# Attention and an MLP on one core: two tiles of batch 0 as block products, values in 64 rows, and another hand-written order

## The chip, the cores and the metric

One core of a Trainium2 chip runs the kernel. The metric is the device time of one launch in microseconds (us); 406.1 us is the median of three runs of the kernel before (405.66 to 406.52).

## The reference

Cosine attention over 8 batches of 12 heads, 448 tokens of 64 features each, and then a two-layer MLP over the 3584 tokens. The MLP's weights are 768 x 2048 and 2048 x 768.

```python
q_n = q / (np.linalg.norm(q, axis=-1, keepdims=True) + 1e-06)
k_n = k / (np.linalg.norm(k, axis=-1, keepdims=True) + 1e-06)
scores = np.matmul(q_n, k_n.transpose(0, 1, 3, 2)) / tau
attn = softmax(scores)
x = np.matmul(attn, v)            # heads side by side: 3584 x 768
h = x @ w_in
g = h * np.clip(h + 3.0, 0.0, 6.0) / 6.0
out = g @ w_out
```

Inputs and output are float32; the matrix products run in bfloat16.

## The kernel before

**Pairs and tiles.** Two heads make a pair, 48 pairs in all, six to a batch. A raw tile j (0 to 47) holds the queries or the keys of two pairs: `load_qk` (line 187) fetches it through SP's DMA queue into a ring of seven buffers, and `raw_before` and `raw_buffer` (135 to 140) turn the ring into one of five from tile 26 on; the two buffers left over then hold intermediate results of the block products (`wide`). `square` (209) squares a tile on ScalarE, POOL or VectorE, `reduce` (226) sums the squares on VectorE, `norms` (244) makes 1/(|x| + 1e-6) of two tiles with four small ScalarE activations, and `normalise` (259) multiplies on POOL or VectorE. `vcast` (278) turns values into bfloat16. Tiles go through TensorE transposes (`transposes`, then copies of queries and keys, `copy_q`, `copy_k`, `copy_k3`) or, from tile 14 on, through the DMA crossbar (`crossbar`).

**Attention.** For a pair, `scores` (388) has four groups: three of two 64-row matmuls each (128 keys of either head), and a fourth for the last 64 keys of both heads. `exps` (421) runs the exponentials on ScalarE: up to pair 5 one instruction for both heads of a group (128 x 896), later one per bank (128 x 448). `values` (446) multiplies the exponentials with the values and a column of ones, eight matmuls of 65 columns a group. For the fourth group they read 64 rows from pair `FIRST` = 18 on, and 128 rows, half of which multiply zeros, before. `finish_values` (466) divides by the sum of the ones column, and `back`, `back_crossbar`, `back_two` bring the result into `xT`, the MLP's input.

**MLP.** `mm1_unit` (560) makes 128 of the 2048 hidden columns for a batch, with six matmuls of 448 columns; ScalarE then makes the gate and VectorE the product (line 581). 16 such units make g of one batch. `mm2_unit` (606) makes half of the output columns for 128 tokens with 16 matmuls of 384 columns. For most of the output a scheme of seven block products (Strassen's, in Winograd's form) takes the place of eight blocks: a pair of 128-token tiles is an entry of `PAIRS` (647), and `product_unit` (720) is one of its seven products, eight matmuls each. The scheme needs sums of blocks of g (`g_sum`, 699, VectorE), sums of blocks of `w_out` (`weight_sums`, 673: "1", "6" and "7" in buffers of their own; "y3" and "y4" written over `w_out` itself, so that ordinary units have to be through with it), and adds of the results on VectorE and POOL. Before, `second` (636) gives batch 0 six ordinary units, and `PAIRS` leaves out its first two tiles (`[1:]`).

**Order.** Each engine works its instructions in program order. Up to pair 17 that order is written out by hand in `PLAN` (line 21): a word is an operation, its number, and the engine (a, v, p for ScalarE, VectorE, POOL). "LQ" and "LV" load, "SQ", "RE", "NO", "NM" make the normalised tiles, "TR" transposes, "SC", "EX", "VA", "FI" are a pair's attention, "U" issues the next unit of a stream whose kinds `ORDER` (19) lists, "UA" and "UV" do the work of ScalarE and VectorE behind a unit, "W" issues one of eight weight DMAs on POOL's queue (the four parts of `w_in`, then the four of `w_out`), and "WS" makes weight sums. "D" and "DP" are fillers: matmuls on zeros into banks that nobody needs (`busy`, `busy_pv`, 913 and 918). From pair 18 on a loop issues the operations, with sums listed per pair in `side` (861). PSUM results from pair 6 on go round a ring of six banks (`next_bank`): a unit or score can start when the bank six places earlier has been read.

```python
for h in (range(2) if name == "M" else ["AB".index(name[0])]):
    rows = slice(64 * h, 64 * h + 64) if name == "M" and i >= FIRST else slice(0, 128)
```

Of the kernel before, what the change touches and what calls it, by code (L numbers as in the profile page):

```python
# [18 lines left out]
ORDER = "111111111111111111111111111111222222"  # L19

PLAN = [
# [40 lines left out]
def kernel(  # L62
# [72 lines left out]
    def raw_before(j):  # L135

        return j - NR if j < 26 else j - NR + 2

    def raw_buffer(j):
        return raws[j % NR if j < 26 else (j - 26) % (NR - 2)]  # L140
# [103 lines left out]
    def norms(d, *items):  # L244
# [11 lines left out]
        for x in items:  # L256
            issued.add(("NO", d, x))
# [185 lines left out]
    def q_cols(b, j):  # L443
        return slice(128 * j, 128 * j + 128)

    def values(i, g):
        needs(("VC", i), ("FI", i - 1), *values_after(i, g))
        at = at_of.pop((i, g))
        vt = vx[i % NVX]
# [643 lines left out]
```

## Time and profile before

| what | us |
|---|---|
| median of three runs | 406.1 |
| the profiled execution | 405.02 |
| its span, first to last instruction | 403.2 |
| first exponential starts | 12.11 |
| first unit of the hidden layer (line 566) starts | 42.09 |
| pair 18's first scores, where the loop starts | 114.64 |
| TensorE's busy share of the span | 98% |

A line of a group or of the timeline gives start and duration in us, the engine, the line of the kernel, the operation, output and inputs by name, shapes and how often; in square brackets stands how long the engine had been idle before, and whom it waited for. Matmuls are pipelined: the duration of one overlaps the next, so the cost of a group is read from its start to the next group's start. The clock column is the share of full speed that TensorE was granted, 1.00 throughout.

### The profile page before, as it was taken

The page shows a single profiled execution, that of the slowest core. Times are in us where ns is not written, and L with a number is a line of the kernel's source. Part 1 is how long each engine was busy: PE and PEld are TensorE (multiplying, and loading weights), DVE is VectorE, ACT ScalarE, POOL GpSimd, SP SyncE. Part 2 cuts the span into 40 slices and gives each one's busy share as a digit, 9 for nine tenths or more (in the row PEclk, how much of TensorE's full clock was granted, in tenths as well). Part 3 has the DMA queues.
Part 4 walks back from the last instruction along what each step waited for, and adds up shares of the span by engine and source line. Part 5 has one row for each costly group of instructions (what it writes and reads, how often), then busy time and mean ns, then how long its engine had stood idle before and what let it go on. Part 6 is the DMA issues. An engine that isn't in the chain of part 4 may idle for free.

```text
span 403.2 us, 9617 instructions
## 1 busy us (share of the span) xinstructions
PE 394.5 (98%) x3696; PEld 233.7 (58%) x3696; DVE 286.4 (71%) x501; ACT 266.2 (66%) x609; POOL 233.2 (58%) x228
## 2 busy tenths in 40 slices
PE   7999999999989999999999999999999999999996
PEld 5666556555655556555555556555565556555564
DVE  6898768766998676776857878687656666644663
ACT  6899998787557686776758768668648755224230
POOL 7899664562294996489386875776665500510070
PEclk9999999999999999999999999999999999999999
DMA  8999989989989559885989659986864523130133
GB/s 290 308 241 276 200 249 239 144 126 221 193 204 231 120 119 228 176 224 130 181 214 210 134 143 171 183 193 145 191 150 82 112 46 67 40 79 20 27 73 99
DMA packets 91566, 65.32 MB, mean 162 GB/s; under 512 B 56064, under 2 KB 89984, under 8 KB 91520
## 3 DMA queue, kind: packets, MB, share of 16 engines
q1 hardware_dynamic: 87408, 58.02, 62.8%
q0 software_dynamic: 3712, 6.29, 9.1%
q8 instruction: 29, 0.48, 0.5%
q10 hardware_dynamic: 400, 0.39, 0.3%
q14 instruction: 17, 0.14, 0.1%
HBM read 47.19 MB, written 11.01 MB: 144 GB/s over the span
## 4 chain that ended last, share of the span: by engine, by line
PE 94%; DVE 3%; DMA 1%; POOL 1%; ACT 0%; issue 0%; SPq 0%; DVEq 0%
PE M L566 24%; PE M L739 17%; PE PV L455 13%; PE Y L566 6%; PE M L415 6%; PE Z L566 5%; PE Y L739 4%; PE Z L739 4%; PE M L613 3%; PE M L819 2%; PE Z L415 2%; PE PV L921 2%; PE Z L819 1%; PE Y L415 1%; PE SC L415 1%; DMA big<-in_q_dram 1%
## 5 line engine op out<-in xcount | busy, mean ns | idle before, releaser
L433 ACT ACTIVATE at<-M 128x448 bf16<-128x448 f32 x200 | 99.6, 565 | 17.7 <-PE M L415 15.5
L566 PE MATMUL M<-xT,w_in_sb 128*128 128x448 bf16 x522 | 110.7, 353 | 0.0
L566 PEld LDWEIGHTS <-w_in_sb 128*128 128x128 bf16 x768 | 71.9, 98 | 62.5 <-issue 2.6
L267 POOL TENSOR_TENSOR nrm<-big,r 128x896 bf16<-128x896 f32 (+1 forms) x48 | 79.4, 1658 | 26.7 <-ACT r L255 18.5
L581 DVE SCALAR_TENSOR_TENSOR gT<-u,M 128x448 bf16<-128x448 bf16 x76 | 46.8, 618 | 35.6 <-ACT u L575 35.3
L455 PEld LDWEIGHTS <-at 128*128 128x128 bf16 (+1 forms) x1536 | 54.8, 97 | 24.1 <-issue 14.8
L224 POOL TENSOR_TENSOR big<-big 128x896 f32<-128x896 f32 (+3 forms) x39 | 63.8, 1639 | 8.0 <-DMA big<-in_k_dram 4.1
L575 ACT ACTIVATE u<-M 128x448 bf16<-128x448 f32 x87 | 48.8, 561 | 29.5 <-PE M L566 29.1
L455 PE MATMUL PV<-vx,at 128*128 128x65 bf16 (+1 forms) x1536 | 64.3, 194 | 0.2 <-DVE on L476 0.2
L236 DVE TENSOR_REDUCE n<-big 128x14 f32<-128x896 f32 (+1 forms) x50 | 51.8, 1040 | 3.9 <-ACT big L222 3.4
L372 POOL COPY km<-tT 64x128 bf16<-64x128 bf16 x34 | 12.4, 364 | 59.3 <-DMA tT<-nrm 43.4
L768 POOL TENSOR_TENSOR big<-big 128x384 f32<-128x384 f32 x11 | 12.0, 1088 | 55.1 <-ACT big L787 55.0
L739 PEld LDWEIGHTS <-gT 128*128 128x128 bf16 x288 | 27.8, 98 | 20.2 <-DVE gT L717 0.6
L739 PE MATMUL M<-w_out_sb,gT 128*128 128x384 bf16 x208 | 37.9, 326 | 0.1
L433 ACT ACTIVATE at<-Z 128x448 bf16<-128x448 f32 x49 | 27.6, 564 | 10.4 <-PE M L415 8.8
L286 POOL CAST vx<-big 128x512 bf16<-128x512 f32 x44 | 33.0, 754 | 2.4 <-DMA big<-in_v_dram 2.4
L476 DVE TENSOR_TENSOR on<-PV,rc 128x512 bf16<-128x512 f32 x48 | 33.2, 691 | 1.7
L415 PE MATMUL M<-tT,kz 64*128 64x448 bf16 (+1 forms) x175 | 31.9, 351 | 1.0 <-DVE o L626 1.0
L739 PEld LDWEIGHTS <-gs 128*128 128x128 bf16 x224 | 21.6, 98 | 14.5
L566 PE MATMUL Y<-xT,w_in_sb 128*128 128x448 bf16 x132 | 28.6, 353 | 0.0
L433 ACT ACTIVATE at<-Y 128x448 bf16<-128x448 f32 x45 | 25.6, 568 | 3.3 <-PE Z L415 3.1
L739 PE MATMUL M<-w_sum,gs 128*128 128x384 bf16 x144 | 26.3, 326 | 0.0
(131 smaller groups left out, 553.9 us busy)
## 6 DMA issues: line engine op xcount, KB each, us to landing
big<-in_v_dram SPq DMA_DIRECT2D x96, 128.0 KB, 4.7
big<-in_k_dram SPq DMA_DIRECT2D x24, 448.0 KB, 4.9
big<-in_q_dram SPq DMA_DIRECT2D x24, 448.0 KB, 4.3
out_dram<-o SPq DMA_DIRECT2D x107, 96.0 KB, 2.2
w_in_sb<-in_moe_w_in_dram POOLq DMA_DIRECT2D x4, 768.0 KB, 9.1
w_out_sb<-in_moe_w_out_dram POOLq DMA_DIRECT2D x4, 768.0 KB, 9.7
tT<-nrm SPq DMA_TRANSPOSE x34, 3.4
xT<-on SPq DMA_TRANSPOSE x25, 3.8
```

What stands on the lines that cost most here:

```text
L224: engines[e].tensor_tensor(out=o, in0=i, in1=i, op=ALU.mult)
L236: nc.vector.tensor_reduce(out=n2s[d % 2][:, j % 2, c], in_=sq[:, :, :, :].rearrange("p g c d -> p (g c) d")[:, c, :], axis=AX.X, op=ALU.add,)
L267: engines[e].tensor_tensor(out=nrm[:, :, g, :].rearrange("p c g d -> p g c d"), in0=raw_of[j][:, g, :, :], in1=rs[d % 2][3][:, j % 2, :] . ...
L286: (engines[e].copy if e == "a" else engines[e].tensor_copy)(out=o, in_=f)
L415: nc.tensor.matmul(o, ks, qt[rows], start=True, stop=True)
L433: nc.scalar.activation(out=o, in_=x, func=AF.Exp, scale=inv_tau)
L455: nc.tensor.matmul(pv_out(j, h), at[rows, n, q_cols(i // HP, j)], vt[rows, 3 + h if name == "M" else 5 * h + int(name[1]), :], start=(name ...
L476: nc.vector.tensor_tensor(out=on[:, :, :, :].rearrange("p j h d -> p h j d"), in0=pv4[:, :, :, 0:D], in1=rc[:, :, :].to_broadcast([128, 2, ...
L566: nc.tensor.matmul(ps[:, 0:S], w_in_sb[:, cc, fc * 128 : (fc + 1) * 128], x[:, cc, 0:S], start=(cc == 0), stop=(cc == CC - 1),)
L575: nc.scalar.activation(out=u[:, :], in_=ps[:, 0:S], func=AF.Relu, bias=0.5, scale=1.0 / 6.0)
L581: nc.vector.scalar_tensor_tensor(out=g[:, fc, c0 : c0 + S], in0=u[:, :], scalar=1.0, in1=ps[:, 0:S], op0=ALU.min, op1=ALU.mult,)
L739: nc.tensor.matmul(m, lhs[:, c, :], rhs[:, c, c0 : c0 + width], start=(base is None and c == 0), stop=(c == KC - 1), skip_group_check=True,)
```

## The change

**Products.** `PAIRS` gains the entry (batch 0, tiles 0 and 1), with the number -1 (`FOREMOST`). `second` now gives batch 0 two ordinary units (tile 2) and seven products of that pair. The sums of g for it are written in the plan ("GS"), the adds on POOL too ("UP").

**Values.** "VA" can carry "h": then the fourth group reads 64 rows. Eleven pairs have it: 1, 6 to 15.

**Norms.** "NA" and "ND" split `norms`: two activations on ScalarE, then an add and a reciprocal on VectorE. Five of the eleven norms of the plan are made so.

**Ring.** The raw ring shrinks to five buffers at tile 19 instead of 26, so that the space for the products' results is free earlier.

**Weight sums.** `weight_sums` can run on POOL; one half of "6" does. All are made in the plan; one half of "y4" was made in the loop (`side`, 18).

**Order.** `PLAN` is written anew. Before it has 10 D and 86 DP fillers, after 10 and 74; tiles 0 and 1 are squared by ScalarE alone; of the normalises of the plan VectorE does 2 before and 8 after, with one of the halves of tiles 0 and 1 each; copies and casts move between VectorE, POOL and ScalarE.

```diff
-ORDER = "111111111111111111111111111111222222"
+ORDER = "111111111111111111111111111111222222222"
...
-    "LQ.1 DP.5 SQ.1.a.11.3 SQ.1.p.4.3 DP.1 SQ.1.a.0.4 LQ.0 SQ.0.p.8.6 DP.2 DP.4 LQ.3 LQ.2 SQ.1.v.7.4 RE.1.1",
-    "SQ.0.a.0.6 RE.1.0 NO.0.1 LQ.5 LQ.4 SQ.0.v.6.2 DP.6 SQ.3.a.0.7 NM.1.p.0 D.10 RE.0.1 DP.3 NM.1.p.1 RE.0.0 DP.8",
-    "NO.0.0 LV.0 DP.2 SQ.2.a.0.7 NM.0.p.0 RE.3 RE.2 NM.0.p.1 TR.1.Y DP.2 TR.0.Z CK.0.v DP.4 SQ.4.p.0.7 CQ.0.v",
-    "SQ.5.a.0.7 LQ.6 NO.1 LV.1 LQ.7 SC.0.0.0 SC.0.1.1 DP.5 DP.3 CQ.1.v EX.0.0 RE.5 RE.4 NM.3.p SC.0.2.0 CK.1.v",
...
+    "D.10 LQ.1 LQ.0 DP.9 DP.2 SQ.1.a.0.2 DP.5 SQ.1.a.2.12 SQ.0.a.0.14 LQ.2 RE.1.0 RE.1.1 NO.0.1 LQ.3 DP.4 RE.0.1",
+    "RE.0.0 LQ.5 NM.1.v.0 NO.0.0 NM.0.v.1 SQ.3.a.0.7 NM.1.p.1 SQ.2.a.0.7 TR.1.Y DP.10 RE.3 LQ.4 CK.0.a NM.0.p.0",
+    "RE.2 SQ.5.a.0.7 TR.0.Z CQ.0.v LQ.6 SQ.4.p.0.7 DP.10 CK.1.v SC.0.0.0 NO.1 SC.0.1.1 EX.0.0 EX.0.1 DP.10 LV.0",
...
-    "CK.17.v XD.18 U EX.16.1 SQ.20.a.0.7 NM.19.p FI.15 WS.6 U UV XD.19 SC.16.3 RE.20 GL.0 WS.1 WS.7.0 EX.16.2 U VA.16.0 UA VA.16.1 LV.11",
-    "EX.16.3 SC.17.0 UV VC.19.p SC.17.1 SC.17.2 SQ.22.v.0.7 VA.16.2 LQ.23 EX.17.0 VA.16.3 EX.17.1 LV.10 U SC.17.3",
-    "XP.14 NO.10 FI.16 NM.20.p CK.18.v U CK.19.v WS.7.1 WS.y3 WS.y4.0 XB.16 EX.17.2 UV UA VA.17.0 VC.18.p EX.17.3 RE.22 CS.18.v",
...
+    "EX.13.1 UA UV NA.8 WS.6.p.0 SC.13.2 UV U UA SC.13.3 EX.13.2 FI.12 VC.14.a CK.14.v U ND.8 VA.13.0 UA U",
+    "NM.17.v UV VA.13.1 EX.13.3 UV W UA NM.16.p VA.13.2 CS.14.v UV SC.14.0 VA.13.3.h LQ.21 SC.14.1 EX.14.0 RE.18",
+    "U U EX.14.1 UA SC.14.2 CK.15.v NO.9 UA EX.14.2 SC.14.3 FI.13 U WS.7.v.0 EX.14.3 UV UV WS.7.v.1 UA VA.14.0",
+    "VC.15.a UV XD.16 VA.14.1 WS.1.v.0 LV.9 SC.15.0 SC.15.1 EX.15.0 U EX.15.1 CK.16.v WS.1.v.1 VA.14.2 XD.17 UA U",
+    "LV.8 GS.-1.6 UA U NM.18.p SC.15.2 EX.15.2 VA.14.3.h SC.15.3 UV SQ.21.a.0.7 WS.6.v.1 LQ.20 WS.y3.v.1 FI.14 UV",
+    "XP.12 CK.17.v U LV.10 UA SC.16.0 SC.16.1 WS.y3.v.0 EX.15.3 WS.y4.v.0 VA.15.0 VA.15.1 EX.16.0 U CS.16.v UA",
+    "VA.15.2 WS.y4.v.1 XD.18 UV VA.15.3.h SC.16.2 U GS.-1.5 EX.16.1 GS.-1.1 VC.17.a VC.16.v UA U GS.-1.2 NM.19.v",
...
-        return j - NR if j < 26 else j - NR + 2
+        return j - NR if j < 19 else j - NR + 2
...
-        return raws[j % NR if j < 26 else (j - 26) % (NR - 2)]
+        return raws[j % NR if j < 19 else (j - 19) % (NR - 2)]
...
+    def powers(d, *items):
+
+        needs(("NM", 2 * d - 4), ("NM", 2 * d - 3))
+        items = items or (0, 1)
+        for x in items:
+            needs(("RE", 2 * d + x))
+        it = slice(items[0], items[-1] + 1)
+        ln, nr = (t[:, it, :] for t in rs[d % 2][:2])
+        nc.scalar.activation(out=ln, in_=n2s[d % 2][:, it, :], func=AF.Ln)
+        nc.scalar.activation(out=nr, in_=ln, func=AF.Exp, scale=0.5)
+        for x in items:
+            issued.add(("NA", d, x))
+
+    def reciprocals(d, *items):
+
+        items = items or (0, 1)
+        for x in items:
+            needs(("NA", d, x))
+        it = slice(items[0], items[-1] + 1)
+        nr, le, r = (t[:, it, :] for t in rs[d % 2][1:])
+        nc.vector.tensor_scalar_add(out=le, in0=nr, scalar1=EPS)
+        nc.vector.reciprocal(out=r, in_=le)
...
-    def values(i, g):
+    def values(i, g, halves=""):
...
-                    rows = slice(64 * h, 64 * h + 64) if name == "M" and i >= FIRST else slice(0, 128)
+                    apart = name == "M" and (i >= FIRST or halves)
+                    rows = slice(64 * h, 64 * h + 64) if apart else slice(0, 128)
...
-        return [(mm2_unit, b, t, m) for m in (1, 0) for t in range(3)]
+        return [(mm2_unit, b, 2, m) for m in (1, 0)] + products(f"3.{FOREMOST} 4.{FOREMOST} 5a.{FOREMOST} 2a.{FOREMOST} 1.{FOREMOST} 6.{FOREMOST} 7.{FOREMOST}")
...
-    def weight_sums(what, c0, n):
+    def weight_sums(what, c0, n, e="v"):
...
-        nc.vector.tensor_tensor(out=o, in0=x, in1=y, op=op)
+        engines[e].tensor_tensor(out=o, in0=x, in1=y, op=op)
...
-        18: [(weight_sums, "y4", KC // 2, KC // 2)], 19: sums(0, "62"), 20: sums(0, "1"),
+        19: sums(0, "62"), 20: sums(0, "1"),
```

More of the change, by code (lines that the diff above doesn't have):

```diff
@@ L255, in norms @@
         nc.scalar.activation(out=r, in_=le, func=AF.Exp, scale=-1.0)
+        for x in items:
+            issued.add(("NO", d, x))
+    def powers(d, *items):
[11 more added lines that the diff above has]
+        items = items or (0, 1)
+        for x in items:
+            needs(("NA", d, x))
[3 more added lines that the diff above has]
+        nc.vector.reciprocal(out=r, in_=le)
         for x in items:
@@ L638, in second @@
         assert b % 2 == 0
-        return [(mm2_unit, b, t, m) for m in (1, 0) for t in range(3)]
+        return [(mm2_unit, b, 2, m) for m in (1, 0)] + products(f"3.{FOREMOST} 4.{FOREMOST} 5a.{FOREMOST} 2a.{FOREMOST} 1.{FOREMOST} 6.{FOREMOST} 7.{FOREMOST}")
     LEFT, RIGHT = slice(0, MH), slice(MH, 2 * MH)
-    PAIRS = [p for b in range(0, B, 2) for p in (((b, 0), (b, 1)), ((b + 1, 3), (b + 1, 0)), ((b + 1, 1), (b + 1, 2)))][1:]
-    LOOP = 8
+    PAIRS = [p for b in range(0, B, 2) for p in (((b, 0), (b, 1)), ((b + 1, 3), (b + 1, 0)), ((b + 1, 1), (b + 1, 2)))]
+    FOREMOST, LAST, LOOP = -1, len(PAIRS) - 2, 8
+    PAIRS = dict(enumerate(PAIRS, FOREMOST))
     summed, g_summed, issued_products = set(), set(), set()
@@ L657 @@
     wide = [big[:, c : c + MH] for c in range(0, 3 * MH, MH)]
-    wide_late = [tail(c, MH) for c in range(TAIL, TAIL + 2 * (len(PAIRS) - LOOP) * MH, MH)]
+    wide_late = [tail(c, MH) for c in range(TAIL, TAIL + 2 * (LAST + 1 - LOOP) * MH, MH)]
     def sum_of(n, what):
@@ L859 @@
     }
-    APART = {(n, y) for n in range(len(PAIRS)) for x, y in (("5a", "3"), ("2a", "4")) if f"{x}.{n}" in " ".join(TURNS.values()).split()}
+    APART = {(n, y) for n in PAIRS for x, y in (("5a", "3"), ("2a", "4")) if n == FOREMOST or f"{x}.{n}" in " ".join(TURNS.values()).split()}
     side = {
-        18: [(weight_sums, "y4", KC // 2, KC // 2)], 19: sums(0, "62"), 20: sums(0, "1"),
+        19: sums(0, "62"), 20: sums(0, "1"),
         21: sums(1, "75"), 22: sums(1, "621"),
@@ L946 @@
     OPS = {
-        "LQ": load_qk, "LV": load_v, "W": next_weights, "SQ": square, "RE": reduce, "NO": norms,
+        "LQ": load_qk, "LV": load_v, "W": next_weights, "SQ": square, "RE": reduce, "NO": norms, "NA": powers, "ND": reciprocals,
         "NM": normalise, "VC": vcast, "TR": transposes, "XD": crossbar, "XB": back_crossbar, "XP": back_two, "CQ": copy_q, "CK": copy_k, "CS": copy_k3, "SC": scores,
-        "EX": exps, "VA": values, "FI": finish_values, "BK": back, "CX": copy_x, "U": unit, "UA": lambda: finish_units("a"), "UV": lambda: finish_units("v"),
-        "GL": g_left, "WS": lambda x, *h: weight_sums(str(x), *((h[0] * KC // 2, KC // 2) if h else (0, KC))), "UU": whole_units, "D": busy, "DP": busy_pv, "OPEN": open_ring,
+        "EX": exps, "VA": values, "FI": finish_values, "BK": back, "CX": copy_x, "U": unit, "UA": lambda: finish_units("a"), "UV": lambda: finish_units("v"), "UP": lambda: finish_units("p"),
+        "GL": g_left, "GS": lambda n, what: g_sum(n, str(what)), "WS": lambda x, e, *h: weight_sums(str(x), *((h[0] * KC // 2, KC // 2) if h else (0, KC)), e), "UU": whole_units, "D": busy, "DP": busy_pv, "OPEN": open_ring,
     }
@@ L955, in do @@
         key = (op,) + tuple(a for a in args if isinstance(a, int))
-        if op not in ("RE", "NM", "LQ"):
+        if op not in ("RE", "NM", "LQ", "NA", "ND"):
             issued.add(key[:3] if op == "SC" else key)
```

2 lines of the change are left out of this document (1 added, 1 removed), and 56 rows, old and new, of the table PLAN.

## The prediction

> **What bounds the kernel now.** I read the page first (busy shares, then the chain that ended last), then the stretches around the change, then single engines there.
>
> ```profile
> PE 394.5 (98%) x3696; PEld 233.7 (58%) x3696; DVE 286.4 (71%) x501; ACT 266.2 (66%) x609; POOL 233.2 (58%) x228
> ...
> PE 94%; DVE 3%; DMA 1%; POOL 1%; ACT 0%; issue 0%; SPq 0%; DVEq 0%
> ```
> The chain is TensorE almost throughout, so what counts is TensorE's work, its waits, and when its real work starts. Four windows (PE, PEld, DVE, ACT, POOL busy; clock; DMA) give the stages: up to the first exponential, up to the first unit of the hidden layer, the rest of the hand-written plan, the loop from pair 18.
>
> ```profile
> 0.00:12.10 12.10, 8.91 (x65) 6.12 (x65) 8.46 (x31) 7.60 (x19) 9.50 (x24) 1.00 0.89 284
> 12.10:42.10 30.00, 29.57 (x420) 19.46 (x419) 25.97 (x60) 28.63 (x57) 28.34 (x24) 1.00 1.07 275
> 42.10:114.60 72.50, 72.50 (x713) 42.19 (x712) 55.69 (x95) 56.11 (x130) 36.93 (x35) 1.00 0.97 196
> ...
> 114.60:403.20 288.60, 283.54 (x2506) 165.94 (x2502) 196.29 (x318) 173.85 (x404) 158.44 (x149) 1.00 0.62 137
> ```
> Up to 42 us TensorE's busy time contains fillers (matmuls on zeros, lines 913 to 922); ScalarE, 28.63 of 30.00, paces. From 42 to 114.6 TensorE has no pause. Then it waits, once, for VectorE's weight sums (line 688), behind which a store copy (L626) stands. TensorE's rows, then VectorE's:
>
> ```profile
> 116.39 0.35 PE L415 MATMUL M<-tT,kz 64*128 64x448 bf16 x1 [1.01 <-DVE o L626]
> ...
> 111.34 4.52 DVE L688 TENSOR_TENSOR w_out_sb<-w_out_sb 128x3072 bf16<-128x3072 bf16 x2
> 115.79 0.54 DVE L626 COPY o<-M 128x384 f32<-128x384 f32 x1
> ```
>
> **1. Products.** Four whole units of 16 matmuls become seven products of 8. The chain prices both:
>
> ```profile
> 104.71 2.60 PE Y L613 x16
> ...
> 121.51 1.30 PE M L739 x8
> ```
> 7 x 1.30 - 4 x 2.60 = -1.30 us of TensorE, in the part without pauses. It costs five sums of g on VectorE (line 717), 0.7 to 1.1 us each, and four POOL adds of about 1.0 (L768 to L780); they lie beside TensorE unless VectorE is late (step 5).
>
> **2. Values in 64 rows.** The plan before runs the last group of values (8 matmuls, line 455) in 128 rows; the loop already runs it in 64, where two row halves overlap. TensorE's rows:
>
> ```profile
> 92.83 0.41 PE L455 MATMUL PV<-vx,at 128*128 128x65 bf16 x8
> 93.17 0.36 PE L415 MATMUL M<-tT,kz 64*128 64x448 bf16 x2
> ...
> 153.99 0.63 PE L455 MATMUL PV<-vx,at 128*128 128x65 bf16 x16
> 154.46 0.35 PE L415 MATMUL Y<-tT,kz 64*128 64x448 bf16 x1
> ...
> 155.12 0.66 PE L455 MATMUL PV<-vx,at 128*128 128x65 bf16 x16
> 155.62 0.35 PE L566 MATMUL Y<-xT,w_in_sb 128*128 128x448 bf16 x1
> ```
> Full groups take 0.25 each (155.12 to 155.62 holds two). Eight before 64-row scores take 0.34 (92.83 to 93.17), so a change of row mode costs about 0.09. In the loop a full group, a change and a half group take 0.47, so the half group takes 0.13: 0.11 saved. All eleven stand beside 64-row scores, so no extra change: -1.2 us (bound: 0 if a change eats it). Nine of them lie behind the first unit: -1.0.
>
> **3. Order on TensorE.** From the two plans I count changes between 64 and 128 rows: 90 before, 82 after; 58 and 46 up to the first unit, 32 and 36 behind it. Behind it that is +4 x 0.09 = +0.4, and two groups of scores now follow it instead of preceding it: +0.4. Work from the first unit on: -1.3 - 1.0 + 0.4 + 0.4 = -1.5 us.
>
> **4. The start.** ScalarE's first exponential starts at 12.11. After, tiles 1 and 0 are squared on ScalarE alone, and VectorE does the reductions of tiles 3 and 2 ahead of the query copy that the first scores need. Tile 1's load lands at 4.24; squares 1.0, two half reductions 1.15, the norms' four steps 1.0, tile 0's norms to 8.6; then squares 3 and 2 at 0.85 each (10.3), two reductions of 1.04 (11.6), the norms of pair 1 (1.03): first exponential at 12.7. Half normalises on VectorE meet POOL's there (step 5), up to +0.9. I take 12.9, 0.8 late; bounds 12.1 to 13.6. Behind it ScalarE decides when the first unit gets a PSUM bank:
>
> ```profile
> 12.11 2.54 ACT L433 ACTIVATE at<-SC 128x896 bf16<-128x896 f32 x3 [0.43 <-PE SC L415]
> ...
> 40.94 1.54 ACT L433 ACTIVATE at<-M 128x448 bf16<-128x448 f32 x3
> ...
> 42.09 0.74 PE L566 MATMUL M<-xT,w_in_sb 128*128 128x448 bf16 x3
> ```
> A wide exponential is spaced 0.80, a single one 0.43. Counting banks along the ring, the first unit reuses that of pair 8's first score before, and of pair 7's third group after: three single exponentials earlier. ScalarE from the first exponential to that read, before: 18 x 0.80 + 21 x 0.43 + 4 norms x 1.03 + one square 0.84 = 28.4 (30.0 passed: 1.6 idle). After: 18 x 0.80 + 18 x 0.43 + one norms 1.03 + two half norms 1.0 + 0.84 + three copies 1.35 + a cast 0.55 = 26.9; with the same idle the first unit is at 12.9 + 28.5 = 41.4: -0.7. Bounds: 39.5 to 43 (+0.9). Fillers behind the first transposes are 55 and 54. The first two weight DMAs keep their place after about the same POOL work; the raw ring of five from tile 19 makes seven loads wait for a normalise two tiles later, and those loads land in 4.3 to 4.9 us, several units ahead of use. The value loads now stand behind the seventh query/key load on SP's queue, ahead of need.
>
> **5. VectorE and POOL.** Through the plan VectorE gains about 8 us (six normalises at 1.09, three casts at 0.68, five sums, reciprocals, less copies), ScalarE about 6, POOL loses about 7. Critical is the end, from the 24th unit to the last: TensorE has 30.4 us (seven hidden units 7.9, two whole units 5.2, seven products 9.1, sixteen score groups 3.0, values 3.8, row changes 1.4); VectorE's list (8 gates 4.4, 4 stores and product adds 2.0, 2 normalises 2.1, 3 reductions 3.1, 5 copies 1.6, 4 value finishes 3.6, 9 half weight sums 8.1, 4 sums of g 2.6, 2 casts 1.3, small ones 0.9) is 29.7. Following it in order, the two in-place weight sums end at about 18 and 19.6, needed at 18.2 and 20.2. So the old stall (1.2 with its resumption) goes, and new waits of 0 to 5 come; I take 1.2. What raises them:
>
> ```profile
> 99.56 1.68 POOL L267 TENSOR_TENSOR nrm<-big,r 128x896 bf16<-128x896 f32 x1
> 101.19 2.14 POOL L286 CAST vx<-big 128x512 bf16<-128x512 f32 x1
> ...
> 100.21 2.65 DVE L688 TENSOR_TENSOR w_sum<-w_out_sb 128x3072 bf16<-128x3072 bf16 x1
> ```
> The weight sum took 2.65, and 1.7 less its wait for POOL's normalise, and POOL's cast then took 2.14 where others take 0.61. [...] One half weight sum goes to POOL: no row; between 0.95 (VectorE's half) and 2.9 (1536/896 x 1.68); I take 2.9, hidden, since POOL has about 13 us of work in those 30.
>
> **Sum.** -0.7 - 1.5 - 1.2 + 1.2 = -2.2 us. The profiled execution took 405.02 (span 403.2 and 1.82 around it); the median is 406.1, so 403.9.
>
> **Rivals.** A: the wait for the last quarter of the output weights. Its DMA stands on POOL behind that half weight sum; the four parts of these weights landed so (shortest, median, longest):
>
> ```profile
> DMA to landing us min/median/max: 7.2/9.7/15.5
> ```
> Half a sum on VectorE needs it at about 8.4 after the 24th unit, and everything up to the block products stands behind. Issued 1 us ahead of that unit and landing after 14.8, it makes VectorE 5.4 us late, TensorE 5 less the old 1.2: 407.7. Slower begins at 4.2 of new waits, a landing of 14 us, or as much of a later issue where the half sum on POOL is dearer. For: VectorE has 0.7 us of slack in 30. Against: POOL idles and may issue earlier. B: exclusion between VectorE and POOL, as in the rows above. Ten two-input instructions of VectorE stand between the 24th unit and the last weight sum, POOL is busy 13 of 30 there, and half of 1.68 is left on average: 10 x 0.43 x 0.84 = 3.6, less 0.6 of slack, 3.0 in place of 1.2: 405.7, no change. For: both engines do more such work at the start too. Against: POOL's total falls by 7. C: the first unit does not come forward (43.0, +0.9 in place of -0.7): 405.5. For: ScalarE was paced at 95% and takes copies and a cast on. Against: the bank count. D: VectorE keeps up and the start is at its early bound: -2.6 - 1.5 - 1.2 = -5.3, 400.8. E: the change doesn't do what it says, 64 rows save nothing: +1.0, 404.9.
>
> **Chances.** Forecast 0.37, D 0.18, E 0.05, C 0.10, B 0.08, A 0.22. Differences under 0.2% (0.8 us; three runs span 0.86) can't be told from none. Faster 0.58 (forecast, D, and most of E), same 0.15, slower 0.27 (A and part of B). The range goes from D to A: 400.7 to 407.7; the forecast's own is 402.3 to 405.2.
>
> **What would show it.** The first L566 at about 41.4 (wrong: 43); seven more rows of 8 L739 matmuls and four units of L613 less; PV rows in 64 rows before pair 18; no wait of TensorE for L626 near the plan's end, and waits for the weight sums or sums of g under 2 us. The forecast is wrong if TensorE waits there 4 us, or if VectorE's two-input rows are much longer than 1.09 and 0.95.

## The result and the profile after

The changed kernel takes 407.83 us, median of 20 runs (405.85 to 411.44, but for one of 571.17 at a granted clock of 0.66, which is left out of the ratio), and the kernel before 405.51 (20 runs on the same chip, 405.02 to 406.81): a ratio of 1.0058, 95% interval 1.0039 to 1.0077. Forecast were 403.9, and a range up to 407.7. The change makes the kernel slower by more than can be mistaken for nothing, in the direction of rival A.

The profile after is of an execution that took 408.87, 1.0 over the median; its span is 406.8, 3.6 us over the 403.2 of before.

First the page: busy shares, then the chain that ended last.

```profile
PE 393.2 (97%) x3676; PEld 232.5 (57%) x3676; DVE 293.0 (72%) x514; ACT 270.7 (67%) x616; POOL 230.7 (57%) x219
...
PE 83%; ACT 6%; DMA 5%; POOL 3%; DVE 2%; issue 1%; SPq 0%; DVEq 0%; POOLq 0%; ACTq 0%
```
TensorE is busy for 1.3 us less than before (393.2 against 394.5) and the span is longer all the same, so it stands idle for longer. TensorE's share of the chain fell from 94% to 83%, and the DMAs' rose from 1% to 5%. The same four windows as before (PE, PEld, DVE, ACT, POOL busy, clock, DMA share, GB/s):

```profile
0.00:12.10 12.10, 9.62 (x61) 6.19 (x62) 8.07 (x29) 8.43 (x19) 6.06 (x20) 1.00 0.87 295
12.10:42.10 30.00, 27.02 (x403) 18.41 (x403) 27.85 (x59) 27.57 (x52) 26.25 (x21) 1.00 1.03 256
42.10:114.60 72.50, 69.83 (x691) 39.56 (x690) 60.62 (x105) 58.13 (x136) 35.71 (x28) 0.98 0.97 194
114.60:406.80 292.20, 286.69 (x2531) 168.32 (x2529) 196.50 (x323) 176.56 (x412) 162.70 (x153) 1.00 0.59 137
```
The third window, without a pause before, has 2.67 us in which TensorE is idle (69.83 busy of 72.50), and some of the clock is lost (0.98). Its rows on TensorE say where (start, length, tile, count, idle time ahead and its releaser):

```profile
93.63 0.41 PE L482 MATMUL PV<-vx,at 128*128 128x65 bf16 x8
96.03 1.56 PE L593 MATMUL M<-xT,w_in_sb 128*128 128x448 bf16 x6 [2.00 <-DVE gT L608]
97.39 4.22 PE L640 MATMUL M<-w_out_sb,gT 128*128 128x384 bf16 x16
...
116.95 2.76 PE L767 MATMUL M<-w_sum,gs 128*128 128x384 bf16 x16 [1.55 <-DVE big L824]
```
Two waits are new, 2.00 and 1.55. Between them the first whole unit takes 4.22 us for its 16 matmuls; 16 matmuls of the same shape take 2.76 in the last row. Windows over that place show that it is the clock (the column ahead of the DMA share, 1.00 and then 0.73 and 0.61):

```profile
94.00:96.00 2.00, 0.04 (x2) 0.00 (x0) 1.51 (x3) 1.29 (x3) 0.00 (x0) 1.00 0.92 86
96.00:98.00 2.00, 1.97 (x8) 0.94 (x8) 1.95 (x3) 0.37 (x1) 0.00 (x0) 0.73 1.06 224
98.00:101.00 3.00, 3.00 (x13) 1.53 (x12) 2.13 (x4) 0.17 (x1) 0.00 (x0) 0.61 1.28 172
```
TensorE's rows name VectorE's gates (L608) and an add of product 1 (L824) as releasers. So the next view is VectorE, then GpSimd:

```profile
91.03 0.61 DVE L608 SCALAR_TENSOR_TENSOR gT<-u,Y 128x448 bf16<-128x448 bf16 x1
94.49 0.96 DVE L716 TENSOR_TENSOR w_sum<-w_out_sb 128x1536 bf16<-128x1536 bf16 x1 [2.85 <-DMA w_out_sb<-in_moe_w_out_dram]
95.37 0.61 DVE L608 SCALAR_TENSOR_TENSOR gT<-u,M 128x448 bf16<-128x448 bf16 x1
...
115.06 0.34 DVE L388 COPY kz<-tT 128x384 bf16<-128x384 bf16 x1
116.34 0.56 DVE L824 TENSOR_TENSOR big<-M,big 128x384 f32<-128x384 f32 x1 [0.94 <-POOL big L797]
```

```profile
80.31 0.80 POOL L937 DMA_DIRECT2D w_out_sb<-in_moe_w_out_dram  x1
81.14 3.11 POOL L716 TENSOR_TENSOR w_sum<-w_out_sb 128x1536 bf16<-128x1536 bf16 x1
84.17 0.78 POOL L937 DMA_DIRECT2D w_out_sb<-in_moe_w_out_dram  x1
...
114.24 0.99 POOL L796 TENSOR_TENSOR big<-big 128x384 f32<-128x384 f32 x1
115.31 0.99 POOL L797 TENSOR_TENSOR big<-big,o 128x384 f32<-128x384 f32 x1
```
Read backwards. VectorE stood 2.85 us at a half weight sum that needs the last quarter of the output weights, with the gate of the next hidden unit behind it, and TensorE behind the gate. That quarter was issued at 84.17, behind a half sum of 3.11 us on GpSimd, and landed 10.2 later, at 94.4, the longest of the four parts:

```profile
DMA to landing us min/median/max: 6.6/9.3/10.2
```
Before, it was issued no earlier (84.70), landed faster (7.2), and nothing on VectorE needed it so soon. The second wait is at product 6. It adds onto the PSUM bank of product 1, so it waits until VectorE has read that bank (L824), and here L824 waits 0.94 for an add on GpSimd (L797).

The account of the 3.6 us is made with three figures of each trace: the first unit's start, the pauses of over 0.4 us behind it (each counted over the usual spacing), and the rest. Start: 42.43 against 42.09, +0.3. Pauses: 4.8 against 1.2, +3.7. The rest of the time from the first unit on is 359.5 against 360.0; in the thirteen runs below that keep the 64-row values and lose no clock there, it is 357.1 to 358.3, median 357.6. So the work is 2.4 less, and the half clock gives 1.9 of it back. 0.3 + 3.7 - 2.4 + 1.9 = 3.5. The split between pauses and the rest depends on what is taken as the usual spacing: with the median spacing of each shape the pauses come to 4.4 and the work to 1.9 less, so a single term is good to half a microsecond.

That account is of one execution, and two of its terms differ from trace to trace. In seven traces with this order up to the first unit (this one and six of the runs below) that unit starts at 42.4 to 45.2, median 43.8: here it is the earliest. In eight traces that leave the last output weights and the sums that need them where the change put them, these weights took 6.7 to 10.4 to land. VectorE stood 2.7 to 3.4 us for them in the three with 9.7 or more, 0.9 in the one with 9.0, and not at all in the four with 6.7 or 6.8. So the wait at 94 is a cost of some executions, and the start costs more than the 0.3 of this one.

### The profile page after: what moved, and what is told of

Its sections match the earlier page's. It is cut to its first block, busy times and chain, and to the rows that moved or that the text cites. A ratio compares the mean times of both kernels' runs of the same rounds, so it can differ in the third digit from the quotient of the medians.

```text
span 569.2 us, 9609 instructions
## 1 busy us (share of the span) xinstructions
PE 561.5 (99%) x3676; PEld 283.3 (50%) x3676; DVE 287.9 (51%) x514; ACT 279.7 (49%) x616; POOL 225.3 (40%) x219
## 3 DMA queue, kind: packets, MB, share of 16 engines
q1 hardware_dynamic: 87408, 58.02, 41.4%
## 4 chain that ended last, share of the span: by engine, by line
PE 97%; DVE 2%; ACT 0%; issue 0%; DVEq 0%
PE M L593 25%; PE M L767 19%; PE PV L482 10%; PE Y L593 8%; PE Z L593 6%; PE Z L767 6%; PE M L441 5%; PE Y L767 4%; PE M L847 3%; PE PV L949 2%; PE Z L441 2%; PE M L640 1%; PE Y L441 1%; PE SC L441 1%; PE Y L944 1%; PE Y L847 1%
## 5 line engine op out<-in xcount | busy, mean ns | idle before, releaser
L593 PE MATMUL M<-xT,w_in_sb 128*128 128x448 bf16 x492 | 153.8, 469 | 0.0
L593 PEld LDWEIGHTS <-w_in_sb 128*128 128x128 bf16 x768 | 88.6, 119 | 113.6 <-issue 104.9
L482 PEld LDWEIGHTS <-at 128*128 128x128 bf16 (+1 forms) x1536 | 66.9, 106 | 32.7 <-issue 22.7
L608 DVE SCALAR_TENSOR_TENSOR gT<-u,M 128x448 bf16<-128x448 bf16 x71 | 44.0, 620 | 74.6 <-ACT u L602 74.5
L482 PE MATMUL PV<-vx,at 128*128 128x65 bf16 (+1 forms) x1536 | 76.2, 209 | 0.0
L225 POOL TENSOR_TENSOR big<-big 128x896 f32<-128x896 f32 x39 | 67.3, 1726 | 12.2 <-DVE n L237 9.0
L767 PE MATMUL M<-w_out_sb,gT 128*128 128x384 bf16 x216 | 57.6, 431 | 0.0
L796 POOL TENSOR_TENSOR big<-big 128x384 f32<-128x384 f32 x12 | 12.4, 1034 | 94.9 <-ACT big L815 94.8
L593 PE MATMUL Y<-xT,w_in_sb 128*128 128x448 bf16 x156 | 49.0, 470 | 0.0
L767 PE MATMUL M<-w_sum,gs 128*128 128x384 bf16 (+1 forms) x168 | 42.6, 420 | 0.5 <-DVE big L824 0.5
L441 PE MATMUL M<-tT,kz 64*128 64x448 bf16 x172 | 40.4, 448 | 0.0
L593 PE MATMUL Z<-xT,w_in_sb 128*128 128x448 bf16 x120 | 38.0, 471 | 0.0
```

The source lines that it names most:

```text
L225: engines[e].tensor_tensor(out=o, in0=i, in1=i, op=ALU.mult)
L441: nc.tensor.matmul(o, ks, qt[rows], start=True, stop=True)
L482: nc.tensor.matmul(pv_out(j, h), at[rows, n, q_cols(i // HP, j)], vt[rows, 3 + h if name == "M" else 5 * h + int(name[1]), :], start=(name ...
L593: nc.tensor.matmul(ps[:, 0:S], w_in_sb[:, cc, fc * 128 : (fc + 1) * 128], x[:, cc, 0:S], start=(cc == 0), stop=(cc == CC - 1),)
L608: nc.vector.scalar_tensor_tensor(out=g[:, fc, c0 : c0 + S], in0=u[:, :], scalar=1.0, in1=ps[:, 0:S], op0=ALU.min, op1=ALU.mult,)
L767: nc.tensor.matmul(m, lhs[:, c, :], rhs[:, c, c0 : c0 + width], start=(base is None and c == 0), stop=(c == KC - 1), skip_group_check=True,)
```

## The experiments

Each edit is of the changed kernel, shown as fragments of its hand-written order unless said otherwise. Ratios are to the kernel before, run on the same chip beside it. One kernel's ratio moves by 0.2% from one group of runs to the next, so a ratio settles the large effects alone, and the small ones are read from the traces, one trace for each kernel.

**The changed kernel again.** No edit.

> The changed kernel as it is, for a profile with TensorE's clock granted in full and for more times. Theory (VectorE is late at the end of the hand-written plan): TensorE waits 4 us or more in all between the 24th unit and pair 18's first iterations, and the first unit of the hidden layer starts near 41.4. Rival 1 (the start): the first unit starts at 43 or later and the waits at the end are under 2 us. Rival 2 (the clock): both are as forecast, the granted clock is under 1.00, and the span is longer by that share alone. Ratio to before 1.004 to 1.008.

Measured: 408.78, 1.0036 (1.0002 to 1.0070). This is the profile shown above: the two large waits of the theory are there, but the first unit, at 42.43, lies between the theory's 41.4 and the 43 of rival 1.

**The last two parts of the output weights 7 to 8 us earlier.**

```diff
-NM.15.p UA VA.11.3.h UV SC.12.1 NM.14.p EX.12.0
+NM.15.p UA W VA.11.3.h UV SC.12.1 NM.14.p W EX.12.0
...
-XD.15 RE.19 W
+XD.15 RE.19
...
-EX.13.3 UV W UA
+EX.13.3 UV UA
```

> The changed kernel with the third and fourth DMA of the output weights issued some 10 us earlier on POOL's queue. If TensorE's loss is the wait of the weight sums for the last quarter of the weights (rival A of the prediction), the kernel becomes 2 to 5 us faster, ratio 0.990 to 0.998, and more even. If VectorE's own work or its exclusion with POOL is the cause, or the start, it stays within 0.7 us of the changed kernel.

Measured: 414.96, 1.0185 (1.0130 to 1.0240), slower where 2 to 5 us less were expected. The wait for the weights is gone, and a larger one stands ahead of its place. GpSimd, VectorE, TensorE in this run:

```profile
84.53 1.68 POOL L225 TENSOR_TENSOR big<-big 128x896 f32<-128x896 f32 x1 [6.07 <-DMA big<-in_q_dram]
...
86.24 1.09 DVE L237 TENSOR_REDUCE n<-big 128x14 f32<-128x896 f32 x1 [4.51 <-POOL big L225]
...
87.91 0.53 PE L441 MATMUL Z<-tT,kz 64*128 64x448 bf16 x1 [4.41 <-DVE gT L608]
```
A raw tile's load is under way together with 1.5 MB of weights and lands 8.0 us after its issue, in place of 4.6; a square on GpSimd waits for it, a reduction for the square, a gate for the reduction. Behind that wait the matmuls are slow (0.53 in the last row, where the same group takes 0.36 in the changed kernel), and the granted clock over the span is 0.986, where the changed kernel's was 0.996. Issue time alone is no free parameter here. That the weights take their time from the tile's load fits these landings; no run shows it apart from the load's later issue (76.0 against 73.6).

**The half sums 8 us later on VectorE.**

```diff
-U WS.7.v.0 EX.14.3 UV UV WS.7.v.1 UA VA.14.0
+U WS.7.v.0 EX.14.3 UV UV WS.1.v.0 UA VA.14.0
...
-VA.14.1 WS.1.v.0 LV.9
+VA.14.1 LV.9
...
-CK.16.v WS.1.v.1 VA.14.2
+CK.16.v VA.14.2
...
-SC.15.3 UV SQ.21.a.0.7 WS.6.v.1
+SC.15.3 UV WS.7.v.1 WS.1.v.1 SQ.21.a.0.7 WS.6.v.1
```

> The changed kernel with the two half weight sums that read the last half of the output weights moved some 8 us later in VectorE's order, behind the gates. Theory (VectorE stands at the landing of the last weights with gates behind it; TensorE waits 2.0 us for a bank, its clock then falls to half for 16 matmuls, 1.7 us): the 2.0 us wait and the rows of matmuls spaced 0.32 are gone, the profiled span falls by about 3.5 us against the changed kernel (to 403 to 404), and the granted clock is 1.00. Rival (VectorE simply has too much work there): the wait comes back a little later at the in-place sums, gain under 1 us.

Measured: 409.31, 1.0085 (1.0059 to 1.0111). The wait near 94 and the half clock there are gone, but TensorE waits at another gate:

```profile
104.49 0.36 PE L441 MATMUL M<-tT,kz 64*128 64x448 bf16 x2 [2.25 <-DVE gT L608]
```
The work that was put off comes due there. Moving it in VectorE's order moves the wait.

**The last output weights ahead of GpSimd's half sum.**

```diff
-NA.8 WS.6.p.0 SC.13.2
+NA.8 W WS.6.p.0 SC.13.2
...
-EX.13.3 UV W UA NM.16.p
+EX.13.3 UV UA NM.16.p
```

> The changed kernel with the last weight DMA issued on POOL ahead of the half weight sum there instead of behind it, 3.1 us earlier. Theory: the landing comes about 3 us earlier, VectorE's wait of 2.85 and TensorE's of 2.0 go, and so does the half clock: 3 to 3.7 us less than the changed kernel. Rival (the transfers share the DMA engines, as in the run with both weights early): the weights land little earlier or the query load of tile 19 lands later, gain under 1 us.

Measured: 407.92, 1.0055 (1.0036 to 1.0073); profile 405.8 at a clock of 1.00. The wait for the weights is gone (issued 83.1, landed 93.2, and VectorE did not stand there), the half clock too. Yet the ratio is that of the changed kernel: in this execution the first unit came at 43.8, product 6 waited 1.4, and TensorE 0.9 for a gate. That the edit removes the wait, and not a quick landing, is borne out by the five traces with the weights first: they took 9.9 to 10.2 to land, and VectorE stood for them in none.

**Products 2 and 5 joined to 4 and 3.** They accumulate on the banks of those products, so that GpSimd has two adds in place of four.

```diff
-GL.0 UP EX.17.0 UP RE.21
+GL.0 EX.17.0 RE.21
...
-products(f"3.{FOREMOST} 4.{FOREMOST} 5a.{FOREMOST} 2a.{FOREMOST} 1.{FOREMOST} 6.{FOREMOST} 7.{FOREMOST}")
+products(f"3.{FOREMOST} 4.{FOREMOST} 5.{FOREMOST} 2.{FOREMOST} 1.{FOREMOST} 6.{FOREMOST} 7.{FOREMOST}")
...
-    APART = {(n, y) for n in PAIRS for x, y in (("5a", "3"), ("2a", "4")) if n == FOREMOST or f"{x}.{n}" in " ".join(TURNS.values()).split()}
+    APART = {(n, y) for n in PAIRS for x, y in (("5a", "3"), ("2a", "4")) if f"{x}.{n}" in " ".join(TURNS.values()).split()}
```

> The changed kernel with the products 5 and 2 of the new pair added onto the banks of 3 and 4, so that POOL has two adds fewer and the chain of adds ahead of product 1's finish is shorter. Theory (TensorE's 1.55 us wait ahead of product 6 is the chain of POOL adds): that wait is gone, about 1.5 us less, perhaps 0.5 given back by products 5 and 2 that wait for ScalarE's copies; the first wait and the half clock stay. Rival (VectorE's order holds product 1's finish): the wait stays at 1 us or more.

Measured: 407.03, 1.0034 (1.0011 to 1.0057). Product 6 waits 0.56 in place of 1.55. But its first unit came at 45.2, 2.8 later than in the profile above, and behind pair 18 it took 1.1 more.

**Joined products and late half sums.** The two edits together.

> Late weight sums and joined products together. If the two waits are separate, the gains add: 4.5 to 5.2 us less than the changed kernel, span 401.5 to 402.5, ratio to before 0.994 to 0.998. If one lateness of VectorE runs through both, the gain is no more than the larger one, ratio 0.998 or more.

Measured: 408.13, 1.0066 (1.0030 to 1.0102). Product 6 waits 1.51 although GpSimd's adds are halved: the adds held L824 for 0.94 in the profile above, but without them the wait stays. L824 stands in VectorE's order behind a reduction, a finish of values and a key copy; the copy began at 115.02 and L824 right behind it, at 115.28, 2.3 us after GpSimd's last add had ended.

**The old order up to the first unit.** The order of before up to its first hidden unit, and from there the changed order, with nine groups of values in 64 rows in place of eleven.

```diff
-    "D.10 LQ.1 LQ.0 DP.9 DP.2 SQ.1.a.0.2 DP.5 SQ.1.a.2.12 SQ.0.a.0.14 LQ.2 RE.1.0 RE.1.1 NO.0.1 LQ.3 DP.4 RE.0.1",
...
+    "LQ.1 DP.5 SQ.1.a.11.3 SQ.1.p.4.3 DP.1 SQ.1.a.0.4 LQ.0 SQ.0.p.8.6 DP.2 DP.4 LQ.3 LQ.2 SQ.1.v.7.4 RE.1.1 SQ.0.a.0.6 RE.1.0",
...
```

> The order of the kernel before up to its first unit, and from there what is left of the changed kernel's order (products, 64 rows, ring and all). Theory (the new start costs 0.3 to 3 us against the old one, from run to run, through VectorE's lateness there): the first unit is back at 42.1 and even from run to run, and the rest costs what it costs in the changed kernel (waits of about 6 us up to pair 18): 1 to 2 us less than the changed kernel in the median. Rival (the start is not to blame): no gain, ratio 1.004 to 1.007.

Measured: 405.24, 0.9990 (0.9967 to 1.0013), 0.7% under the changed kernel. The first unit starts at 42.16, the last output weights land at 89.4, after 6.8, so that VectorE has no wait for them, and product 6 still waits 1.4. What goes with the changed start reaches further than the first unit: between 82 and 88 us TensorE waits 0.4 to 1.1 for a gate in nine of the thirteen traces with it, and at most 0.3 in the three with the old one.

**Tile 5 normalised on GpSimd.** In the changed start VectorE normalises tile 5 while GpSimd normalises another tile; the key copy behind it is late (shown below, at the unexpected rows).

```diff
-NM.4.p SQ.6.a.0.7 NM.5.v SC.1.0.0
+NM.4.p SQ.6.a.0.7 NM.5.p SC.1.0.0
```

> The changed kernel with one normalise, that of tile 5, on POOL instead of VectorE. Theory (it took 2.63 us in place of 1.08 because POOL's normalise of tile 4 ran, and TensorE waited 1.2 to 1.9 for the key copy behind it): that wait falls under 0.5 and the first unit comes 0.7 to 1.5 us earlier. Rival (VectorE is late there from the work ahead of it, whatever the exclusion): it stays at 1 us or more, and POOL's later squares make it worse.

Measured: 407.17, 1.0035 (1.0002 to 1.0067). TensorE's wait for that copy is gone, and the first unit waits:

```profile
41.07 0.36 PE L441 MATMUL M<-tT,kz 64*128 64x448 bf16 x2
43.12 1.30 PE L593 MATMUL Y<-xT,w_in_sb 128*128 128x448 bf16 x6 [1.68 <-ACT at L459]
```
The releaser named is ScalarE, but its read of that bank ended at 41.0. It is the other need of this unit, the second part of the input weights: issued at 31.68 (before: 28.01), landed at 42.98.

**That DMA directly behind the first.**

```diff
-CQ.7.v W EX.4.1 SC.4.2.0 SQ.10.p.0.7
+CQ.7.v W W EX.4.1 SC.4.2.0 SQ.10.p.0.7
...
-CQ.6.v W CX.2.v
+CQ.6.v CX.2.v
```

> The changed kernel, with the second DMA of the input weights issued directly behind the first on GpSimd's queue, ahead of the two squares and the normalise that stood between them. Theory (the first unit waits for the landing of these weights, which the new order issued 4.5 us later): the DMA is issued at about 28 to 29 us and lands at 38 to 41, the first unit starts at 41.4 to 42.0 where ScalarE releases its bank, and the kernel takes 0.4 to 1.0 us less than the changed one, about 407.2; the wait for the output weights near 94 us stays. Rival (the bank or the bandwidth decides, not the issue): the first unit stays at 42.4 or later, or TensorE pauses ahead of it for a raw tile whose load the weights delay, and the time stays at 407.8 or rises.

Measured: 407.14, 1.0054 (1.0029 to 1.0078). Issued at 25.74, landed at 39.31, and the first unit still at 43.64: the rival holds. Here the key copy's wait (1.57) is still there, TensorE's clock is low behind it (0.94 over the second window), and ScalarE releases the bank at 43.26. Two causes stand one behind the other, and each hides the other.

**The values in 128 rows again.** All eleven `VA.x.3.h` become `VA.x.3`.

> The changed kernel with the last key group's values of all eleven pairs in 128 rows again, nothing else. Theory (step 2 of the prediction): each of these groups takes about 0.34 us in place of 0.12 to 0.23 between 64-row scores, 0.11 to 0.22 more; nine of them lie behind the first unit, so the stretch from the first unit to pair 18 takes about 1.0 us more work, and the kernel about 1.0 us more, 408.8, unless waits shrink in turn. Rival (E of the prediction, 64 rows save nothing): the values' rows take the same time and the kernel 407.8.

Measured: 407.94, 1.0063 (1.0039 to 1.0086). Between two groups of scores, this kernel:

```profile
88.56 0.36 PE L441 MATMUL M<-tT,kz 64*128 64x448 bf16 x1
88.86 0.42 PE L482 MATMUL PV<-vx,at 128*128 128x65 bf16 x8
89.21 0.36 PE L441 MATMUL M<-tT,kz 64*128 64x448 bf16 x2
```
And the changed kernel at the same group:

```profile
86.81 0.36 PE L441 MATMUL M<-tT,kz 64*128 64x448 bf16 x1
87.01 0.28 PE L482 MATMUL PV<-vx,at 64*128 64x65 bf16 x8
87.13 0.35 PE L441 MATMUL M<-tT,kz 64*128 64x448 bf16 x2
```
From the group's first matmul to the next scores it is 0.35 against 0.12. The rest without pauses is 359.5 against 357.6: 64 rows save 1.9 us behind the first unit, and nine groups at 0.23 make 2.1. The time does not show it (1.0063 against 1.0058 and 1.0036 with 64 rows): the pauses behind the first unit are 2.4 here against 4.8, though part of that is that the last weights landed after 9.0.

**Old start, joined products and the last weights first.** And the same **without the joined products**.

> Old start, last weight DMA ahead of the half weight sum, and products 5 and 2 on the banks of 3 and 4: all three costs taken away. Theory: first unit at 42.1, 72.5 to 73.5 from there to pair 18, 287.3 behind it: span 402 to 403, ratio to before 0.995 to 0.999. If the waits only change place, the ratio is 1.001 or more.

> The order of before up to the first unit, then the changed order, with the last DMA of the output weights ahead of the half weight sum on GpSimd; products 2 and 5 apart, as in the changed kernel. Theory (what made the changed kernel slow is the start's later weight DMA and the wait for the output weights; joining products cost about 1.1 us in the loop): first unit at 42.1, stretch to pair 18 about 72.0, the rest 287.0, a span of 401.2, and a median of about 404.0, ratio 0.994 to 0.998. Rival (the wait moves to product 6's bank and VectorE's later work, as in the kernel with the weights first alone): 405 to 405.5, no faster than before.

Measured: 404.70, 0.9985 (0.9960 to 1.0011), and 404.63, 0.9974 (0.9963 to 0.9985). The second is faster than both kernels. All of TensorE's waits for VectorE at product 6's line come to 1.8 there, none is for weights, and its rest without pauses is 357.1.

**Both repairs of the start.** Tile 5 on GpSimd and the two input-weight DMAs side by side; and the same with the last output weights first.

> The changed kernel with two edits in the start at once: tile 5 normalised on GpSimd in place of VectorE (alone, this took away the wait for the key copy near 20 us, but the first unit then waited 1.68 for the input weights), and the second DMA of the input weights issued directly behind the first (alone, this left the first unit at 43.64, behind ScalarE's bank). Theory (both hold the first unit, one behind the other, and the bank count of the prediction was right): no wait of TensorE over 1 us and no half clock from 15 to 43 us, and the first unit at 41.1 to 41.8, with a time about 1 us under the changed kernel's; the wait for the output weights near 94 us stays. Rival (the start is held by something that neither edit touches, such as ScalarE's own pace): first unit at 42.4 or later.

> The same, with the last DMA of the output weights ahead of the half weight sum on GpSimd as well. Theory (start and weight wait are separate and add up): first unit at 41.1 to 41.8, no wait for the output weights, the stretch from the first unit to pair 18 about 74.5 or less, and a time of 405 to 406. Rival (a repaired start only moves the wait to later work, since VectorE and GpSimd pace the middle): first unit early, but the stretch to pair 18 longer by as much, 407 or more.

Measured: 411.38, 1.0154 (1.0101 to 1.0206), and 411.63, 1.0159 (1.0142 to 1.0177). Both theories fall: a new wait of 3.99 stands at 29 us. VectorE, GpSimd and TensorE of the first of the two:

```profile
28.18 5.03 DVE L293 TENSOR_TENSOR nrm<-big,r 128x896 bf16<-128x896 f32 x1
...
27.29 3.33 POOL L225 TENSOR_TENSOR big<-big 128x896 f32<-128x896 f32 x2
30.57 1.68 POOL L293 TENSOR_TENSOR nrm<-big,r 128x896 bf16<-128x896 f32 x1
...
33.27 0.93 PE L338 MATMUL Y<-ident,nrm 128*128 128x128 bf16 x7 [3.99 <-DVE nrm L293]
```
A normalise that took 1.08 in the changed kernel takes 5.03. Its end, 33.21, less those 1.08 is 32.13: by this estimate VectorE's work on it began when GpSimd's three instructions in a row ended, at about 32.2. In the changed kernel GpSimd stood idle for 0.53 ahead of its second square, waiting for a reduction, and the normalise began 0.16 before that square.

**The DMA between the two squares**, with tile 5 on GpSimd; and the same with the last output weights first.

```diff
-SC.4.2.0 SQ.10.p.0.7 BK.2.Z
+SC.4.2.0 SQ.10.p.0.7 W BK.2.Z
...
-CQ.6.v W CX.2.v
+CQ.6.v CX.2.v
```

> The changed kernel with tile 5 normalised on GpSimd, and the second DMA of the input weights issued between the two squares behind the first one, as before the change, in place of behind the normalise that follows them. Unlike the two DMAs side by side, this leaves a gap between GpSimd's two-input instructions at about 27.5 us, where VectorE's normalise of tile 6 stands. Theory (bank count right; the key copy's wait and the weight DMA held the first unit, and the 4 us wait of the last try was VectorE's normalise shut out by three two-input instructions of GpSimd in a row): that normalise takes under 2 us, the DMA is issued at 27 to 28 and lands at 39 to 41, no wait of TensorE over 1 us from 15 to 43, the first unit at 41.2 to 41.8. Rival (a late weight DMA or its load on the others delays something else again): first unit at 42.4 or later, with another wait ahead of it.

> The same, with the last DMA of the output weights ahead of the half weight sum on GpSimd. Theory (start and middle add up): first unit at 41.2 to 41.8, no wait for the output weights, the stretch to pair 18 74.0 to 75.0, a time of 404.5 to 405.5, about as before the change. Rival (the middle takes back what the start gives, since VectorE's list there is full): stretch to pair 18 of 75.5 or more and 406 or more.

Measured: 407.14, 1.0028 (1.0003 to 1.0053), and 405.78, 0.9974 (0.9949 to 0.9999), with 406.30 for the kernel before on that chip. The normalise takes 1.10 in both. In the first the weights, issued at 28.70, land only at 43.41, and the first unit waits 0.94 for them; in the second they land at 41.23 and the unit starts at 42.59 behind its bank. From the first exponential (13.66) that is 28.9. The second trace's middle, first unit to pair 18, is 74.5, where the changed kernel's was 77.5. By its median the second kernel, the changed start repaired at two places with the output weights issued first, reaches the ratio that the old start with the weights first gave: slightly faster than before. The two traces don't say where its gain over the first comes from, since in the first the output weights landed after 6.7 and nothing waited for them.

## Why the prediction was wrong

**Step 1, products: held.** A product's 8 matmuls are spaced 1.31 in the plan, as priced. What the step left open, "unless VectorE is late", came true: product 6 waited 1.4 to 1.6 in every trace but one (0.56). The prediction had the adds and the sums, but not that product 6 needs product 1's bank, and that the read of it stands last in a full list.

**Step 2, 64 rows: right in kind, too small.** 1.9 us measured where 1.0 was forecast behind the first unit. The price left out that a group in 128 rows between scores also brings the row changes back: the prediction's own rows had 0.34 for such a group and 0.13 for one in 64 rows, and the traces show 0.35 and 0.12, so 0.23 a group, not 0.11. Rival E is out.

**Step 3 and the work: held, too small.** Work from the first unit on: forecast -1.5, measured -2.4 (-1.9 with the other spacing), by the term of step 2. The part behind pair 18 went from 288.6 to 286.9 with the old stall.

**Step 4, the start: failed in its second half.** The first exponential came at 12.95 in the profile shown (forecast 12.9) and at 12.4 to 13.7 in the runs that keep this start. The bank count held as well: forecast 28.5 from there to the first unit, 28.9 measured where nothing else held it. What failed is the time at which the bank and the weights were there. One step of it is "The first two weight DMAs keep their place after about the same POOL work". The second was issued at 32.5 in place of 28.0, behind two squares and a normalise on GpSimd, and landed at 42.13; in the run that freed the bank earlier, the first unit waited 1.68 for it. The other is the wait of 1.19 for a key copy, which was not foreseen: the prediction gave half normalises up to 0.9 for their meeting with GpSimd's, and not the whole one of tile 5, which took 2.63. So the first unit came at 42.43, not 41.4. In that profile it is the bank that decided: the unit starts 0.38 behind the end of ScalarE's read, as in two runs where the weights had long landed, and the weights, 0.3 before the unit, stood ready as the next to hold it. Rival C had an outcome of this kind (43.0, and six of the seven traces with this start are later than that), with ScalarE's copies as its reason; the runs show the key copy's wait, half the clock behind it in five of the seven, and the weights instead.

**Step 5, the end of the plan: failed.** The old stall went, as forecast. New waits were put at 1.2 and came to 4.8 in the profile shown, and the half clock behind the first of them added 1.9. The failed step is the sum that followed VectorE's list "in order" without the landing of the last weights, which took 10.2 there and held VectorE for 2.85. Rival A described that wait, line by line: the DMA behind GpSimd's half sum (3.11; 2.9 was estimated), VectorE's half sum at its landing, everything behind it. Its price was another: 2.0 on TensorE, not 5, since the DMA landed 9.4 us after the end of its issue, where the prediction counted 14.8 in the same way. Rival A held 14 us to be needed for slower; 9.4 was enough in this execution, because the product's wait, the clock and the later start came on top. In four of the eight traces the weights landed in time, so rival A is part of the cause and the start is the other part. Issuing this DMA first takes the wait away, but alone does not win the time back (1.0055). The old start alone nearly does (0.9990), and with both repairs the kernel is faster than before (0.9974).

**Rival B** happened at the start: two meetings of normalises cost 2.56 on GpSimd, where VectorE began first (13.19 against 13.27), and 2.63 on VectorE, where GpSimd did; with three of GpSimd's in a row it was 5.03. Between the 24th unit and the last weight sum, where it was priced, the rows show no such lengths on VectorE (0.95, 0.96, 1.08), so its 3.0 was not spent there.

What stays open: why the same 768 KB of weights land after 6.6 us at one time and after 14.7 at another (15.5 before the change). With more of them issued at once a tile's load landed later, but no run separates bandwidth from the issue on GpSimd. How often the last weights land late over many executions isn't known: there is one trace for each kernel. Single edits that repair one wait are not told apart by the ratios (1.0028 to 1.0066); which wait costs how much rests on the traces.

## What to carry to other kernels

Price a moved DMA by its landing, for every transfer that is issued behind the moved work, and check what that landing holds one stage later; one weight DMA was issued 4.5 us later than before and one 0.5 earlier, they landed 2.0 and 2.5 us later, and each could hold TensorE. When several waits stand close together, repair them together before judging an edit: alone, three sound repairs left the ratio at 1.0035 to 1.0055. A landing time that changes from execution to execution needs more than one trace. And where VectorE and GpSimd share such work as the normalises and squares here, look at which of GpSimd's instructions follow each other at once: moving one DMA issue to another place in its queue turned a normalise of 1.10 into 5.03.

## What the runs showed that was not expected

**VectorE's normalise of 1.08 took 2.63 beside one instruction of GpSimd, and 5.03 beside three in a row.** The changed start, on VectorE, GpSimd and then TensorE:

```profile
16.99 2.63 DVE L293 TENSOR_TENSOR nrm<-big,r 128x896 bf16<-128x896 f32 x1
...
16.98 1.69 POOL L293 TENSOR_TENSOR nrm<-big,r 128x896 bf16<-128x896 f32 x1 [0.60 <-DVE r L281]
...
21.27 0.36 PE L441 MATMUL SC<-tT,kz 64*128 64x448 bf16 x2 [1.19 <-DVE kz L360]
```
GpSimd began 0.01 earlier, and VectorE's 1.08 became 2.63, 0.1 less than GpSimd's 1.69 and its own together. With three of GpSimd's in a row it became 5.03, and TensorE waited 3.99 for it in both kernels with that order. It is not always so. In the run with only tile 5 moved, two squares of GpSimd stood next to each other, on VectorE and GpSimd:

```profile
27.45 1.10 DVE L293 TENSOR_TENSOR nrm<-big,r 128x896 bf16<-128x896 f32 x1
...
25.90 4.19 POOL L225 TENSOR_TENSOR big<-big 128x896 f32<-128x896 f32 x2
```
The first square ended at 27.59, and the second began 0.02 later and took 2.48, where the first took 1.69; VectorE, begun 0.14 before the first one's end, took 1.10. In the run with 5.03 each of GpSimd's instructions is recorded as begun before the one ahead of it ended; yet the cast that followed the three just as closely, at 32.21, took 1.48 in place of 0.61, and VectorE's normalise ended within it. What decides is not shown.

**Behind a pause of 2.0 us the clock was at half, and behind one of 2.6 it was not.** Behind 2.00 us of idle at 94 the granted clock was at half for 3.4 us (0.73 over two and 0.61 over three us in the windows above), which loses 1.7, or 1.9 by the account above; with tile 5 on GpSimd, TensorE was idle for 2.56 at the same place, and no matmul behind it was slow (the 16 of the next whole unit took 2.76). Near 20 us eight traces have a pause of 1.2 to 1.8 at the key copy; behind six of them the clock was at half for a while (with the second weight DMA directly behind the first, two matmuls of scores at 23.57 took 0.56 in place of 0.36), behind two (1.19 and 1.60) it was not. So a pause's length alone doesn't decide it here; what does is not shown.

The clock column reads 1.00 where there is no record, and the spacing of the matmuls there says otherwise: up to 5.2 us before and 8.2 us after, fillers of 248 columns are spaced 0.21 and behind it 0.11, as at half the clock. Only fillers run there.

**GpSimd's half weight sum** took 3.11 us where VectorE's took 0.95, and the last DMA of the weights, behind it in GpSimd's order, was issued at 84.17, 3.0 after the sum began.
